# A fused chunk-attention and bilinear-FFN kernel: block 1's output as seven half products, W_out's sums between casts, unit 5's transposes by DMA, and a few moved steps

## The chip, the core and the metric

The kernel runs on one core of a Trainium2 chip. The time is the device time of one execution in microseconds (us), and the figure that is compared is the median over runs. A core has five engines that run their own instruction streams in order: PE (matmuls), DVE (vector), ACT (scalar activations), POOL (GpSimd) and SP, which here only issues DMAs. They meet through semaphores.

## What is computed

Eight sequences of 576 tokens with 8 heads of 64 features go through attention within chunks of 64 tokens, and the result, 4608 rows of 512, goes through a bilinear feed-forward layer with 1536 hidden features.

```python
def _attn_ref(q, k, v):                      # (8, 8, 576, 64) each
    q_c, k_c, v_c = (t.reshape(8, 8, 9, 64, 64) for t in (q, k, v))
    scores = np.matmul(q_c, k_c.transpose(0, 1, 2, 4, 3)) / np.sqrt(64)
    attn = np.exp(scores - np.max(scores, axis=-1, keepdims=True))
    attn = attn / (np.sum(attn, axis=-1, keepdims=True) + 1e-09)
    return np.matmul(attn, v_c).reshape(8, 8, 576, 64)

def _moe_ref(x, w_a, w_b, w_out):            # x (4608, 512), w_a, w_b (512, 1536), w_out (1536, 512)
    return ((x @ w_a) * (x @ w_b) @ w_out).astype(np.float32)
```

## The kernel before

**Units and blocks.** Rows are worked on in 18 units of 256 rows for the attention and in 9 blocks of 512 rows (two units) for the feed-forward layer. The whole order of all five engines is written out by hand (`tc.manual_schedule`): each call appends its instructions to the streams of the engines it uses, so the place of a call in the source is its place in every one of those streams.

**Attention of a unit U.** `load` issues the DMAs of q, k and v from SP. `cast` turns them into bf16 on POOL (`k_raw` and so on, L203). q and k are then transposed into `qkt`, in one of two ways. For units below `PE_UNITS` they are loaded in pieces of 512 bytes, transposed on PE (`transpose_pe`, L217, eight 128x128 tiles each for q and k) and copied out of PSUM by DVE and ACT (L225). For the others they are loaded in the natural order in pieces of 256 bytes and transposed by a DMA issued from SP (`transpose_dma`, L230). `scores` (L248, exponentials on ACT at L256), `sums` (L263, logarithms at L273), `inverse` (L282, the reciprocal as an exponential) and `values` (L296, the product with the reciprocal on DVE at L305, written to `xT`) follow. `bring(U)` casts q and k, loads q of unit U+1, transposes U by DMA, casts v and loads k and v of U+1. SP runs these DMAs in that order.

**Feed-forward.** Block 0 is done by `ab_step` (L355): 12 steps of plain products, 512 columns each. Block 1 is done by 24 half steps `h` of 256 columns, which need only unit 2 for the first twelve. From block 2 on, `Group` uses a scheme with seven products in place of eight (p1 to p7, L405), which needs sums of the weights (`combine_w`, on DVE, L129, four parts for each of six pieces) and sums of x (`combine_x`, on DVE, L385, four parts). The scheme's PSUM copies are on ACT, its additions and its final multiplication on DVE (L443, L444, L455).

**Output.** Block K's output is made while block K+1's products run. Block 0 uses `out_0`, four groups of 12 plain matmuls of 512 columns (L609), in block 1's stretch. Block 1 does the same in pieces of four matmuls (`out_part`), twelve pieces set between block 2's products. From block 2 on, `OutGroup` uses the scheme of seven products for the output too: 14 half products of six matmuls of 256 columns (L541). It needs sums of W_out (`combine_wo`, on POOL, L158, four parts of three) and sums of the hidden product (`combine_ab`, on POOL, L485, four parts of three). Part 3 of `combine_wo` overwrites a quarter of W_out, so it must come after the last plain product that reads it. `chunks` says how many of these pieces stand at each of the twelve places of a block.

The sums of W_out stand in the POOL stream of blocks 2 and 3:

```python
if K == 2:
    for _ in range(2 if i < 3 else 1):
        combine_wo(*wo_sums.pop(0))
if K == 3 and i == 1:
    while wo_sums:
        combine_wo(*wo_sums.pop(0))
```

Of the kernel before, what the change touches and what calls it, by code (L numbers as in the profile page):

```python
# [8 lines left out]


PE_UNITS = 6
AB_SCALE = 256.0
OUT_SCALE = 1.0 / AB_SCALE

# [2 lines left out]
def kernel(  # L17
# [10 lines left out]
    nc = tc.nc  # L28
# [292 lines left out]
        if f is not None:  # L321
            values(f)

    def bring(U):

        if U >= NU:
            return
        cast(U, "qk")
        load(U + 1, "q")
        if U < NU:  # L330
            transpose_dma(U)
        cast(U, "v")
        load(U + 1, "kv")


    ab_tiles = {}

# [281 lines left out]
    with tc.manual_schedule(  # L619
        engines={  # L620
            mybir.EngineType.PE,
            mybir.EngineType.SP,
            mybir.EngineType.DVE,
            mybir.EngineType.Activation,
            mybir.EngineType.Pool,
        }
    ):

        load(0, "qk")
        load(1, "qk")  # L630
        load(0, "v")
        load(1, "v")
        for i in range(3):
            load_ab(i)
        cast(0, "qk")
        transpose_pe(0)
        cast(1, "qk")
        cast(0, "v")
        cast(1, "v")
        cast_ab(0)  # L640
        load_ab(3)
        cast_ab(1)
# [24 lines left out]
        for j in range(6):  # L667
            load_wo(j)
        for j in range(6):
            cast_wo(j)  # L670
        load(4)
        load(5)
        spread[:] = [psum_t, psum_t, psum_a, psum_q]
        combos = [(i, p) for i in range(NWP) for p in range(3)]

        def combo():
            if combos:
                combine_w(*combos.pop(0))

        for ft in range(NFT):  # L680
            ab_step(0, ft)
            if 3 <= ft < 10:
                combo()
            if ft == 6:
                transpose_pe(2)
            if ft == 8:
                slot(2)
            if ft == 10:
                slot(None, 2)

        cast(4)
        cast(5)
        load(6)

        outs = []

        def chunk(n=1):
            for _ in range(min(n, len(outs))):
                outs.pop(0)()

        def half(ft, u):
            ab_step(1, ft, 256 * u, 256 * u + 256)
            if ft > 9 if u == 0 else ft != 5 and ft != 9 and ft != 11:
                combo()
            if u == 1 and ft % 2 and ft > 2:
                combine_w(ft // 2 - 1, 3)

        halves = [(ft, u) for u in range(2) for ft in range(NFT)]

        def h(n=1):  # L710
            for _ in range(n):
                half(*halves.pop(0))

        def normalize(U):
            sums(U)
            inverse(U)

        def out_0(tg):
            for p in range(3):
                out_part(0, tg, p, psum_b)  # L720

        spread[:] = [psum_t, psum_b]
        h(1)
        transpose_pe(3)
        h(3)
        scores(3)
        h(3)
        normalize(3)
        h(2)
        values(3)  # L730
        bring(6)
        h(8)
        out_0(0)
        transpose_pe(4)
        h(2)
        scores(4)
        out_0(1)
        transpose_pe(5)
        h(1)
        normalize(4)  # L740
        h(1)
        scores(5)
        h(1)
        values(4)
        bring(7)
        h(1)
        spread[:] = [psum_a, psum_q]
        normalize(5)
        out_0(2)
        spread[:] = [psum_t]  # L750
        values(5)
        combine_x(2)
        h(1)
        out_0(3)
        assert not halves and not combos

        attention = {}
        for K in range(2, NBLK):
            U = 2 * K + 2
            for at, f, u in (  # L760
                ((0, 0) if K == 2 else (-1, 1), scores, U),
                ((0, 1) if K == 2 else (0, 0), sums, U),
                ((1, 0), inverse, U),
                ((1, 1), values, U),
                ((2, 1), scores, U + 1),
                ((3, 0), sums, U + 1),
                ((3, 1), inverse, U + 1),
                ((4, 1), values, U + 1),
                ((5, 0), lambda u: combine_x(u // 2, (0, 1)), U + 1),
            ):  # L770
                if u < NU:
                    at = (K - 1, NWP - 1, 1) if at[0] < 0 else (K, *at)
                    attention[at] = [lambda f=f, u=u: f(u)]

        for K in range(3, NBLK):
            attention.setdefault((K, 0, 0), []).insert(0, lambda K=K: combine_x(K, (2, 3)))

        def attend(K, i, n):
            for f in attention.get((K, i, n), ()):
                f()  # L780

        wo_sums = [(p, j) for p in range(4) for j in range(3)]
        last = None
        chunks = {
# [3 lines left out]
            NBLK - 1: (1,) * 12,  # L788
        }

        def finish(g):

            K, i = g.K, g.i
            if K >= 2 and i >= 3:
                for part in (0, 1, 2):
                    combine_ab(K, part, i - 3, nc.vector if (K, i) == (NBLK - 1, 5) else None)

        for K in range(2, NBLK):
            for i in range(NWP):
                if i == 1:  # L800
                    if K == 2:
                        outs += [
                            lambda tg=tg, p=p: out_part(1, tg, p, (psum_o, psum_q)[tg % 2])
                            for tg in range(4) for p in range(3)
                        ]
                    else:
                        for j in range(3):
                            combine_ab(K - 1, 3, j)
                if i in (1, 3):
                    bring(2 * K + 4 if i == 1 else 2 * K + 5)  # L810
                if K == 2:
                    for _ in range(2 if i < 3 else 1):
                        combine_wo(*wo_sums.pop(0))
                if K == 3 and i == 1:
                    while wo_sums:
                        combine_wo(*wo_sums.pop(0))
                if K == 2 and i == 0:
                    combine_w(NWP - 1, 3)
                if K > 2 and i == 0:
                    g = OutGroup(K - 1)  # L820
                    outs += [
                        lambda g=g, n=n, th=th: g.part(n, th) for n in range(7) for th in range(2)
                    ]
                now = Group(K, i)
                now.p1()
                if last:
                    last.add7()
                chunk(chunks.get(K, chunks[4])[2 * i])
                if last:
                    last.p3()  # L830
                attend(K, i, 0)
                now.p6()
                if last:
                    last.p4()
                    finish(last)
                now.p2()
                chunk(chunks.get(K, chunks[4])[2 * i + 1])
                attend(K, i, 1)
                now.p5()
                now.p7()  # L840
                last = now
        ends = [
            OutGroup(NBLK - 1, 0, (psum_t, psum_q, psum_o)),
            OutGroup(NBLK - 1, 1, (psum_t, psum_b, psum_a)),
        ]
        last.add7()
        ends[0].part(0, 0)
        last.p3()
        ends[1].part(0, 1)
# [39 lines left out]
```

The softmax here doesn't subtract the row's maximum and nothing guards it: scores larger than these inputs give would overflow.

## Time and profile before

Four runs took 310.65 to 311.82 us, median 311.15 us. The profiled execution is the one of 311.82 us.

| | profiled execution |
|---|---|
| time of that execution | 311.82 us |
| span from first to last instruction | 310.0 us |
| granted PE clock | 0.999 |
| PE busy | 293.4 us (95%) |
| DVE, ACT, POOL busy | 206.8, 194.1, 178.2 us |
| DMA moved | 54.03 MB, 174 GB/s on average |
| packets under 512 bytes | 114016 of 138887 |

A row of a timeline gives the start in us from the span's start, the duration, the engine, the line, the operation and its tiles, and in brackets how long the engine was idle before it and what released it. Matmuls overlap at their ends, so durations of neighbours add up to more than the clock shows; the distance from start to start is what a group costs. In the page's second part each digit is one fortieth of the span, in tenths.

### The profile page before, as it was taken

Reading aid. Unit: us, or ns where it says so; the run is one execution under the profiler, and the core shown is the slowest. Engines: PE = TensorE matmul, PEld = TensorE weight load, DVE = VectorE, ACT = ScalarE, POOL = GpSimd, SP = SyncE. Lnnn points to the kernel's source line nnn. Section 1 sums busy time; section 2 is a strip of 40 time slices with the busy share of each in tenths; the row PEclk is TensorE's granted clock in tenths of the full one; section 3 lists DMA queues with packets and bytes.
Section 4 is the critical chain, followed back from the end, with each engine's and each line's share of the span. In section 5 each row is a group of like instructions: output and inputs, shape, how many; then the busy total and the mean of one; then the engine's idle time right before and its main releaser. Section 6 shows DMA issues by size and latency. Waiting matters only on the chain.

```text
span 310.0 us, 8487 instructions
## 1 busy us (share of the span) xinstructions
PE 293.4 (95%) x3478; PEld 228.6 (74%) x3478; DVE 206.8 (67%) x342; ACT 194.1 (63%) x350; POOL 178.2 (57%) x168
## 2 busy tenths in 40 slices
PE   2889889999999999999999999999999999999995
PEld 1534457866566768888888888888888888888884
DVE  3446663975866687567757776777668766965872
ACT  1743557448575657666877687768676867566531
POOL 1565656554348588945782678277737711780560
PEclk9999999999999999999999999999999999999999
DMA  7999899999999993699539953994492000300015
GB/s 233 307 377 277 246 340 339 209 246 200 269 224 220 241 253 92 85 231 242 139 63 239 242 140 74 218 273 121 93 182 103 36 0 2 137 1 3 0 75 197
DMA packets 138887, 54.03 MB, mean 174 GB/s; under 512 B 114016, under 2 KB 132960, under 8 KB 138848
## 3 DMA queue, kind: packets, MB, share of 16 engines
q1 hardware_dynamic: 138704, 53.36, 70.2%
q8 instruction: 27, 0.44, 0.6%
q10 hardware_dynamic: 144, 0.13, 0.1%
q14 instruction: 12, 0.10, 0.1%
HBM read 37.75 MB, written 9.44 MB: 152 GB/s over the span
## 4 chain that ended last, share of the span: by engine, by line
PE 75%; DMA 7%; DVE 7%; POOL 5%; ACT 3%; issue 2%; SPq 1%; DVEq 0%; POOLq 0%; ACTq 0%
PE pb L405 17%; PE pc L405 11%; PE pa L405 10%; PE po L541 9%; PE pq L541 8%; DMA st<-in_moe_w_b_dram 3%; PE pb L609 3%; DMA st<-in_k_dram 2%; DVE s L385 2%; PE po L355 2%; PE pc L355 2%; DMA st<-in_q_dram 2%; POOL so L485 2%; PE pa L355 2%; PE pq L355 2%
## 5 line engine op out<-in xcount | busy, mean ns | idle before, releaser
L405 PEld LDWEIGHTS <-t 128*128 128x128 f16 x504 | 48.3, 98 | 10.1 <-issue 4.1
L443 DVE TENSOR_TENSOR c_sb<-pc,v_sb 128x512 f32<-128x512 f32 x42 | 28.8, 686 | 35.0 <-ACT v_sb L416 34.3
L485 POOL TENSOR_TENSOR so<-ab_sb 128x512 f16<-128x512 f16 x20 | 23.0, 1152 | 50.3 <-DVE ab_sb L455 50.3
L405 PE MATMUL pb<-s,wa 128*128 128x256 f16 x336 | 50.6, 273 | 0.1
L405 PE MATMUL pa<-xT,wb 128*128 128x256 f16 x336 | 50.4, 273 | 0.0
L416 ACT COPY u_sb<-pb 128x512 f32<-128x512 f32 x42 | 24.7, 587 | 24.8 <-PE pb L405 23.5
L541 PEld LDWEIGHTS <-ab_sb 128*128 128x128 f16 x336 | 32.9, 98 | 4.2 <-issue 0.4
L405 PEld LDWEIGHTS <-wb 128*128 128x128 f16 x336 | 32.9, 98 | 4.0
L203 POOL CAST k_raw<-st 128x1024 bf16<-128x1024 f32 x17 | 17.9, 1056 | 30.9 <-DMA st<-in_k_dram 26.4
L405 PEld LDWEIGHTS <-wa 128*128 128x128 f16 x336 | 31.0, 98 | 6.2 <-issue 0.2
L455 DVE SCALAR_TENSOR_TENSOR ab_sb<-pc,c_sb 128x512 f16<-128x512 f32 x42 | 28.9, 688 | 6.9 <-PE pc L405 5.5
L455 DVE SCALAR_TENSOR_TENSOR ab_sb<-pb,b_sb 128x512 f16<-128x512 f32 x42 | 28.9, 687 | 3.0 <-PE pb L405 2.6
L423 ACT COPY pb<-pa 128x512 f32<-128x512 f32 x42 | 24.6, 587 | 8.5 <-PE pa L405 8.4
L416 ACT COPY v_sb<-pb 128x512 f32<-128x512 f32 x42 | 24.9, 592 | 8.1 <-PE pb L405 8.1
L416 ACT COPY b_sb<-pa 128x512 f32<-128x512 f32 x42 | 25.0, 595 | 7.7 <-PE pa L405 7.7
L444 DVE TENSOR_TENSOR pc<-pc,u_sb 128x512 f32<-128x512 f32 x42 | 29.0, 689 | 0.0
L203 POOL CAST v_raw<-st 128x1024 bf16<-128x1024 f32 x18 | 19.0, 1057 | 15.7 <-DMA st<-in_v_dram 11.8
L305 DVE TENSOR_TENSOR xT<-pt,ln 128x512 f16<-128x512 f32 x30 | 19.4, 685 | 12.2 <-PE pt L296 12.2
L541 PEld LDWEIGHTS <-so 128*128 128x128 f16 x252 | 24.6, 98 | 3.4 <-issue 0.5
L405 PE MATMUL pc<-s,t 128*128 128x256 f16 x168 | 25.2, 272 | 0.6 <-DVE ab_sb L455 0.6
L405 PE MATMUL pb<-s,t 128*128 128x256 f16 x168 | 25.3, 273 | 0.4 <-DVE ab_sb L364 0.4
L405 PE MATMUL pc<-xT,t 128*128 128x256 f16 x168 | 25.2, 272 | 0.1
(132 smaller groups left out, 572.4 us busy)
## 6 DMA issues: line engine op xcount, KB each, us to landing
out_dram<-o_sb SPq DMA_DIRECT2D x34, 256.0 KB, 3.3
st<-in_v_dram SPq DMA_DIRECT2D x32, 256.0 KB, 4.2
st<-in_q_dram SPq DMA_DIRECT2D x23, 256.0 KB, 4.8
st<-in_k_dram SPq DMA_DIRECT2D x23, 256.0 KB, 3.6
st<-in_moe_w_b_dram SPq DMA_DIRECT2D x6, 512.0 KB, 7.6
st<-in_moe_w_a_dram SPq DMA_DIRECT2D x6, 512.0 KB, 8.0
st<-in_moe_w_out_dram SPq DMA_DIRECT2D x6, 512.0 KB, 6.7
st<-in_q_dram SPq DMA_DIRECT2D x4, 512.0 KB, 5.9
```

What stands on the lines that cost most here:

```text
L203: eng.tensor_copy(out=raw[n, U], in_=staged.pop((n, U)))
L305: nc.vector.tensor_tensor(out=x.rearrange("p m (g c s) -> p m g c s", g=2, c=2)[:, :, :, cl, :], in0=av[cl], in1=rs[:, cl].rearrange("p m ...
L355: nc.tensor.matmul(ps[n], w_ab[n, i][:, kt, o:o + 128], xT[:, kt, c0:c1], start=(kt == 0), stop=(kt == NKT - 1),)
L405: nc.tensor.matmul(t[:, h * 256:h * 256 + 256], w[:, kt, h * 128:h * 128 + 128], x[:, kt], start=start and h == 0 and kt == 0, stop=h == 1 ...
L416: nc.scalar.copy(out=t, in_=src)
L423: nc.scalar.copy(out=self.B, in_=self.A)
L443: nc.vector.tensor_tensor(out=self.c, in0=self.C, in1=self.v, op=ADD)
L444: nc.vector.tensor_tensor(out=self.C, in0=self.C, in1=self.u, op=ADD)
L455: nc.vector.scalar_tensor_tensor(out=self.dst[:, :, c0:c0 + 256], in0=t.rearrange("p (h n) -> p h n", h=2), scalar=AB_SCALE, in1=o.rearran ...
L485: (eng or nc.gpsimd).tensor_tensor(out=o, in0=x0, in1=x1, op=op)
L541: nc.tensor.matmul(t[:, c0:c0 + 256], a[:, kt, th * 128:th * 128 + 128], w[:, kt], start=n in (0, 4) and first and kt == 0, stop=last and ...
L609: nc.tensor.matmul(out_ps[K, tg], ab_tiles[K][:, ft, tg * 128:tg * 128 + 128], wo_sb[:, ft], start=(ft == 0), stop=(ft == NFT - 1),)
```

## The change

- `PE_UNITS` goes from 6 to 5. Unit 5's q and k are loaded in natural order and transposed by DMA; its 16 PE transposes and their four copies go.
- `bring` takes a part of `combine_wo` and puts its three pieces between its casts: `bring(5, 0)` in place of `cast(4)`'s follower `cast(5)` and `load(6)`, and `bring(6, 1)`. Part 3 of W_out's sums now stands at the start of block 2, part 2 at its third pair of products; none is left in block 3.
- Block 1's output uses `OutGroup` like the later blocks: 14 half products in block 2. Its `combine_ab` parts 0 to 2 stand at half steps 7, 9 and 11 of the second half of block 1, part 3 in block 2.
- In block 0, `sums(2)` and `inverse(2)` move one step ahead of `values(2)`; unit 3's q is transposed ahead of block 1's first half step and its k after it.
- Unit 5's sums use the banks `psum_q` and `psum_o` in place of `psum_a` and `psum_q`. The last half step of block 1 stands ahead of x's sums for block 2, whose parts 2 and 3 move to the start of block 2. One matmul on zeros into `psum_q` (whose result nothing reads) stands ahead of `out_0(3)`.
- Part 3 of `combine_w` for the pieces 3, 4 and 5 moves into block 2's first three pairs.

```diff
-PE_UNITS = 6
+PE_UNITS = 5
...
-        cast(U, "qk")
+        def between(j):
+            if part is not None:
+                combine_wo(part, j)
+
+        cast(U, "q")
+        between(0)
+        cast(U, "k")
         load(U + 1, "q")
-        if U < NU:
-            transpose_dma(U)
+        transpose_dma(U)
+        between(1)
         cast(U, "v")
         load(U + 1, "kv")
-
+        between(2)
...
+            if ft == 9:
+                sums(2)
+                inverse(2)
             if ft == 10:
-                slot(None, 2)
+                values(2)
...
         cast(4)
-        cast(5)
-        load(6)
+        bring(5, 0)
...
-            if u == 1 and ft % 2 and ft > 2:
+            if u == 1 and ft in (3, 5, 7):
                 combine_w(ft // 2 - 1, 3)
+            if u == 1 and ft % 2 and ft > 6:
+                for part in range(3):
+                    combine_ab(1, part, ft // 2 - 3)
...
+        transpose_pe(3, "q")
         h(1)
-        transpose_pe(3)
+        transpose_pe(3, "k")
...
-        bring(6)
+        bring(6, 1)
...
-        transpose_pe(5)
...
-        spread[:] = [psum_a, psum_q]
+        spread[:] = [psum_q, psum_o]
         normalize(5)
         out_0(2)
         spread[:] = [psum_t]
         values(5)
-        combine_x(2)
         h(1)
+        combine_x(2, (0, 1))
+        whole = bank(psum_q)
+        nc.tensor.matmul(whole, warm_in[:, :128], warm_in, start=True, stop=True)
         out_0(3)
...
-        for K in range(3, NBLK):
+        for K in range(2, NBLK):
             attention.setdefault((K, 0, 0), []).insert(0, lambda K=K: combine_x(K, (2, 3)))
...
-            2: (0, 0, 1, 1, 1, 1, 1, 1, 1, 1, 1, 1),
-            3: (1, 1, 2, 2, 1, 1, 2, 2, 1, 1, 1, 1),
+            2: (0, 1, 1, 1, 2, 1, 2, 2, 1, 1, 1, 1),
...
-                if i == 1:
+                if K == 2 and i == 0:
+                    combine_wo_all(3)
+                if i == (2 if K == 2 else 1):
+                    for j in range(3):
+                        combine_ab(K - 1, 3, j)
                     if K == 2:
-                        outs += [
-                            lambda tg=tg, p=p: out_part(1, tg, p, (psum_o, psum_q)[tg % 2])
-                            for tg in range(4) for p in range(3)
-                        ]
-                    else:
-                        for j in range(3):
-                            combine_ab(K - 1, 3, j)
+                        combine_wo_all(2)
...
-                if K == 2:
-                    for _ in range(2 if i < 3 else 1):
-                        combine_wo(*wo_sums.pop(0))
-                if K == 3 and i == 1:
-                    while wo_sums:
-                        combine_wo(*wo_sums.pop(0))
-                if K == 2 and i == 0:
-                    combine_w(NWP - 1, 3)
-                if K > 2 and i == 0:
+                if K == 2 and i < 3:
+                    combine_w(i + 3, 3)
+                if i == 0:
                     g = OutGroup(K - 1)
```

More of the change, by code (lines that the diff above doesn't have):

```diff
@@ L322, in slot, with bring @@
             values(f)
-    def bring(U):
+    def bring(U, part=None):
         if U >= NU:
             return
-        cast(U, "qk")
+        def between(j):
[4 more added lines that the diff above has]
+        cast(U, "k")
         load(U + 1, "q")
-        if U < NU:
-            transpose_dma(U)
+        transpose_dma(U)
+        between(1)
         cast(U, "v")
         load(U + 1, "kv")
+        between(2)
     ab_tiles = {}
@@ L687, with combine_wo_all @@
                 slot(2)
+            if ft == 9:
+                sums(2)
+                inverse(2)
             if ft == 10:
-                slot(None, 2)
+                values(2)
+        def combine_wo_all(part):
+            for j in range(3):
+                combine_wo(part, j)
         cast(4)
-        cast(5)
-        load(6)
+        bring(5, 0)
         outs = []
@@ L780, in attend @@
                 f()
-        wo_sums = [(p, j) for p in range(4) for j in range(3)]
         last = None
         chunks = {
[2 rows of a table removed]
+            2: (0, 1, 1, 1, 2, 1, 2, 2, 1, 1, 1, 1),
             4: (1, 1, 1, 1, 1, 1, 2, 2, 1, 1, 1, 1),
@@ L799 @@
             for i in range(NWP):
-                if i == 1:
-                    if K == 2:
-                        outs += [
-                            lambda tg=tg, p=p: out_part(1, tg, p, (psum_o, psum_q)[tg % 2])
-                            for tg in range(4) for p in range(3)
-                        ]
-                    else:
-                        for j in range(3):
-                            combine_ab(K - 1, 3, j)
+                if K == 2 and i == 0:
+                    combine_wo_all(3)
+                if i == (2 if K == 2 else 1):
+                    for j in range(3):
+                        combine_ab(K - 1, 3, j)
+                    if K == 2:
+                        combine_wo_all(2)
                 if i in (1, 3):
                     bring(2 * K + 4 if i == 1 else 2 * K + 5)
-                if K == 2:
-                    for _ in range(2 if i < 3 else 1):
-                        combine_wo(*wo_sums.pop(0))
-                if K == 3 and i == 1:
-                    while wo_sums:
-                        combine_wo(*wo_sums.pop(0))
-                if K == 2 and i == 0:
-                    combine_w(NWP - 1, 3)
-                if K > 2 and i == 0:
+                if K == 2 and i < 3:
+                    combine_w(i + 3, 3)
+                if i == 0:
                     g = OutGroup(K - 1)
```

## The prediction

> **What bounds the kernel now.** I read the page's busy shares first, then its forty slices, then PE's timeline from block 0's end to block 3 for every place where PE was idle, and last the SP and POOL streams, which say when the data for those places can be there.
>
> ```profile
> PE 293.4 (95%) x3478; PEld 228.6 (74%) x3478; DVE 206.8 (67%) x342; ACT 194.1 (63%) x350; POOL 178.2 (57%) x168
> PE   2889889999999999999999999999999999999995
> DMA  7999899999999993699539953994492000300015
> ```
>
> PE is busy 95% of the span and almost without a gap from 135 us to the tail at the end. So the end moves by what PE's own work loses or gains, and by what its idle places lose or gain. The DMA row shows the second limit: up to about 112 us the DMA engines are full, afterwards not. The edit lies in 38 to 135 us, partly where both are full.
>
> ```profile
> 44.18 0.60 PE L355 MATMUL pa<-xT,wb 128*128 128x256 f16 x4 [1.47 <-DVE xT L305]
> ...
> 70.20 0.61 PE L217 MATMUL pt<-identity,q_raw 128*128 128x128 bf16 x8
> 70.65 0.61 PE L217 MATMUL pb<-identity,k_raw 128*128 128x128 bf16 x8
> 71.10 0.60 PE L355 MATMUL pq<-xT,wb 128*128 128x256 f16 x4
> ...
> 76.78 0.41 PE L263 MATMUL pa<-E,ones 64*64 64x512 bf16 x2 [0.47 <-ACT v_sb L363]
> ...
> 85.01 0.60 PE L405 MATMUL pb<-s,t 128*128 128x256 f16 x4 [0.37 <-DVE ab_sb L364]
> ...
> 87.79 1.03 PE L609 MATMUL po<-wo,ab_sb 128*128 128x512 f16 x4
> 88.65 0.60 PE L405 MATMUL pb<-s,wa 128*128 128x256 f16 x4
> ...
> 114.02 0.60 PE L405 MATMUL pc<-s,t 128*128 128x256 f16 x4 [0.41 <-DVE ab_sb L455]
> ...
> 126.28 0.82 PE L541 MATMUL pq<-wot,so 128*128 128x256 f16 x6
> 126.93 0.60 PE L405 MATMUL pb<-s,wa 128*128 128x256 f16 x4
> ...
> 132.03 1.03 PE L541 MATMUL pq<-wo,so 128*128 128x256 f16 x8 [0.30 <-POOL wo L158]
> ```
>
> These are PE's timeline: its idle places that the edit touches (1.47, 0.47, 0.37, 0.41, 0.30 us), unit 5's transposes (70.20 to 71.10), and the price of an output piece from start to start: 0.86 us for four plain matmuls, 0.65 for six half ones.
>
> ```profile
> 72.23 2.43 SPq L230 DMA_TRANSPOSE qkt<-q_raw  x1
> 74.76 1.25 SPq L230 DMA_TRANSPOSE qkt<-k_raw  x1
> 76.06 2.09 SPq L176 DMA_DIRECT2D st<-in_k_dram  x2
> ```
>
> This is SP: unit 6's two transposes, and the load queued behind them. Unit 6's k landed at 79.01, 6.8 us after 72.23.
>
> **The change part by part.** All in the profiled execution (span 310.0, time 311.82); that run is 0.67 above the median of 311.15, so I carry the difference over to the median.
>
> *Block 0's end.* PE waits 1.47 us at 44.18 because sums(2) came at 40.16, its logarithms and reciprocal took ACT until 42.81 and DVE's two products ran from 42.84 to 44.13. With sums(2) one step (1.73 us) earlier, at 38.4, ACT works 38.9 to 41.0. But ACT's copy v_sb of step 10 is now queued behind them: 41.0 to 41.6, and DVE's multiplication of that step 41.6 to 42.2 stands ahead of the xT products, which run 42.2 to 43.5. Block 1 starts at 43.55, not 44.18: 0.63 us. v of unit 2 was cast by 40.02 and values(2) now comes at 40.45, q of unit 3 was cast by 41.78 and is transposed at 42.6 inside the remaining gap: 0.45 us more (45.05 to 45.50 before). Sum -1.08; between -0.5 (the transposes alone) and -1.5 (the gap gone).
>
> *Unit 5's transposes off PE.* -0.90 (70.20 to 71.10); its four copies, 1.34 us on DVE and 1.33 on ACT, were beside other work. PE would reach scores(5) at 73.39 - 1.98 = 71.41.
>
> *Unit 5's transposes in SP's queue.* Now q5 and k5 are four DMAs of 256 KB with 256-byte packets, not two of 512 KB. In the trace a 256 KB load lands 0.9 to 1.0 us after the one before it, a 512 KB one with 512-byte packets 1.5 us after (k5, 62.22 to 63.73): +0.9 us on this queue. q6's last piece was issued by 66.25; now by 67.2, and the q transpose follows it at once, since q5 (landing near 62.7) and k5 (64.5) are cast on POOL by 66, with one W_out sum between. From the q transpose's issue to the k transpose's landing the twelve pairs took 4.1 us (190 us, empty queue) to 6.8 (72 us, full). This queue is full, but the loads just ahead are of 128 KB; I take 5.9, the 83 us pair, so 73.1. PE waits from 71.41 to 73.15: +1.74; from 0 (4.1 us) to 3.9 (start 68.5, 6.8 us). So scores(5) starts at 73.15 where it was 73.39: of 1.98 us gained, 0.24 stays.
>
> [...] The trace has PE at 0.90 us for all 16 tiles, and a DMA pair in a full queue adding 1.95 us (q8 landed 87.19, unit 7's transposes 88.30 and 89.14). [...] The rows are of the same operation in this kernel, so I take 5.9 us.
>
> *Sums(5) and the zero matmul.* Sums(5) waited 0.47 us for ACT's copy v_sb out of pa. Now it needs u_sb, one copy earlier, and DVE's read of po; with ACT and DVE 1.3 us lighter and 2.3 us of PE between scores(5) and it, the wait goes: -0.47 (0 if DVE is late). The zero matmul needs pq after ACT's copy c_sb, which ended at 81.2 when PE was free at 81.08; it takes 0.22: +0.4 (0.2 to 0.5). From scores(5) to block 2's scores(6) was 10.81 us (73.39 to 84.20) and becomes 10.74: scores(6) at 83.9.
>
> *What is late next: unit 6.* k6's load stands behind unit 5's transposes on SP. They end issuing 3.8 us after their start (as at 72.23 to 76.01), at 71.0; k6, v6 and q7 took 5.9 us to issue (66.35 to 72.23): 76.9; plus 6.3: k6's transpose lands at 83.2. Scores(6) needs it at 83.9. Slack 0.7; before it was 5.2.
>
> *POOL.* k6 and v6 would land near 75.6 and 77.5. POOL does v6's cast and the last sum of part 1 by 80, then the first two `combine_ab` triples (three of 1.16 us) by 87, the three casts of unit 7 by 90.1 (q7 was cast at 75.78; its transpose at SP's turn, about 87.5, thus waits 0.6 us, and unit 7 is needed at 96.9 with a landing near 94), the third triple, whose second sum is ready at 92.5. PE asks for it in the fifth chunk of block 2, at 94. Part 3 of W_out's sums (three of 1.13) ends at 97 and is asked for at 98.9; `combine_ab` part 3 ends at 103.5, asked for at 105; W_out's part 2 at 107, asked for at 110. Four slacks of 1.5 to 3 us. Stores of block 1's output go behind unit 9's transposes in SP's order, which are due late (scores(9) stood at 129.43). For unit 6 and POOL together I put +0.2 (0 to 3).
>
> *Block 2's PE work.* Twelve pieces of 0.864 us become fourteen of 0.655: 10.37 - 9.17 = -1.20. ACT gets five copies of 0.58 us more and DVE one operation of 0.68 less, as in the later blocks, where PE has no gap. x's sums stand behind one DVE multiplication and, parts 2 and 3, behind one weight sum: with each at the slow 1.26 us of this trace, s2 is ready 4.3 us after values(5), asked for after 4.8. The 0.37 us at 85.01 is ACT's copy of pa and stays. The three moved weight sums are used from the fourth pair on.
>
> *Two waits.* At 114.02 DVE was behind by an o_sb eviction (L602, 0.59 us on its path) that is gone: -0.4. At 132.03 PE waited for W_out's part 3 on POOL, now done 35 us earlier: -0.3.
>
> Sum: -0.24 - 0.47 + 0.4 - 1.20 - 0.4 - 0.3 + 0.2 = -2.0 us. Profiled 311.8 becomes 309.8; the median 309.1.
>
> **The rivals.** *The transpose is in time* (chance 0.2): with 4.1 us the k transpose lands at 71.3 and the 1.74 us are kept: -3.75, 307.4. For it: pieces just ahead are small. Against: no pair below 110 us took less than 5.9.
>
> *The gain is only moved* (0.13): pair at 6.8 us and a start at 68.5, landing at 75.3: -2.0 + 2.15 = +0.15, 311.3; anything between that and 0.9 less is no change.
>
> *Slower: unit 6's keys* (0.15). Place: scores(6), block 2's start. Unit 6's transposes follow unit 5's in one queue and so carry its lateness twice, and everything that POOL casts after k6 comes later with them. It decides from the k transpose landing after 83.9; each us then costs one; at 86.8 the sum is +0.9, at 88 it is +2.1, 313.3. For it: the slack falls from 5.2 to 0.7 and DMA is at 1.0 to 1.2 in this stretch. Against: the time at which unit 6 is due moves with PE's own wait. [...]
>
> *Not as written:* that block 1's output still waits for its sums in block 2, so that the 1.2 us are given back in POOL waits; it is in the 0.2 above, and at 1.5 us it gives 310.4, still inside.
>
> **How the numbers follow.** Likeliest, 0.52: -2.0, own range 308.2 to 310.1. In time: 0.20, about 307.4. Only moved: 0.13, 310.2 to 311.5. Slower: 0.15, above 312. A measurement of this kernel can tell about 0.3%, 0.93 us, from no change: faster means under 310.2, slower over 312.1. Faster: 0.72; same: 0.13; slower: 0.15. The range leaves out the slower case and the tip of the in-time one: 307.2 to 311.2.
>
> **What would show it.** Right: block 1 starts near 43.6 with unit 3's q before it; PE idle before scores(5) by 1 to 2.5 us with a DMA as releaser; no wait at unit 5's sums; no L609 in block 2; no idle at block 3's 132. Wrong: scores(5) without a wait (307.4); PE idle at scores(6) or in L541 of block 2 with POOL so or wot as releaser; a clock under 1.0.

## The result: a little faster, less than half of the forecast

The changed kernel took 309.99 us in the median (308.76 to 312.35 over 43 runs); the kernel before, run beside it, 311.15 us (309.98 to 312.98 over 64). The ratio of the means (310.31 and 311.19 us) is 0.9972, with a 95% interval of 0.9961 to 0.9982: 0.9 us faster (1.2 us by the medians), where 2.0 had been forecast. A second batch (c0 below) gave 0.9981 (0.9966 to 0.9995). The profiled execution of the changed kernel took 310.67 us, with a span of 308.9 us.

The page of the changed kernel, first its busy time and then two rows of its forty slices:

```profile
PE 293.0 (95%) x3499; PEld 231.4 (75%) x3499; DVE 209.5 (68%) x339; ACT 195.9 (63%) x353; POOL 192.3 (62%) x180
PE   2879999999999989999999999999999999999995
DMA  7999999999989998399639943993493000300025
```

PE has as much to do as before. What grew is POOL, from 178.2 to 192.3 us (twelve `combine_ab` sums for block 1's output), and DVE, from 206.8 to 209.5 us, although three DVE instructions fewer are issued; ACT's 1.8 us more are its additional copies. On DVE, fewer instructions in more time: some of them became slower. That is the first hint.

PE's timeline at the places that the prediction named:

```profile
43.38 0.60 PE L362 MATMUL pa<-xT,wb 128*128 128x256 f16 x4 [0.19 <-DVE xT L305]
...
69.79 0.60 PE L362 MATMUL pq<-xT,wb 128*128 128x256 f16 x4
...
72.07 0.22 PE L248 MATMUL pt<-qkt 64*64 64x64 bf16 x2
...
75.64 0.40 PE L263 MATMUL po<-E,ones 64*64 64x512 bf16 x2 [0.28 <-DVE ab_sb L371]
...
80.12 0.38 PE L771 MATMUL pq<-warm_in 128*128 128x512 bf16 x1
80.34 2.75 PE L616 MATMUL pb<-wo,ab_sb 128*128 128x512 f16 x12
...
89.75 0.60 PE L412 MATMUL pc<-xT,t 128*128 128x256 f16 x4 [0.51 <-DVE pc L451]
...
114.72 0.60 PE L412 MATMUL pc<-s,t 128*128 128x256 f16 x4 [0.83 <-DVE ab_sb L462]
```

The gap ahead of block 1 fell from 1.47 to 0.19 us. Scores(5), at 72.07, did not wait for its DMA in this execution. But PE now waits for DVE at 75.64, 89.75 and 114.72, and the last wait, which was to go, has doubled (0.41 before). The 0.30 us at block 3's 132 are gone. SP's queue:

```profile
65.70 1.97 SPq L230 DMA_TRANSPOSE qkt<-q_raw  x1
67.77 1.24 SPq L230 DMA_TRANSPOSE qkt<-k_raw  x1
69.06 1.95 SPq L176 DMA_DIRECT2D st<-in_k_dram  x3
...
74.78 2.88 SPq L230 DMA_TRANSPOSE qkt<-q_raw  x1
```

Unit 5's pair was issued at 65.70 (forecast 67.2) and its k landed at 71.26 (forecast 73.1). Behind it stand unit 6's loads, from 69.06 on.

**A ledger by stretches.** Executions of one kernel differ by a microsecond or more, and much of that comes from the start: scores(2), with nothing ahead of it changed, began between 35.35 and 37.10 us in all but one of the kernels below. So I count in PE's timeline from scores to scores, from the first matmul of one unit's scores to that of a later unit's. The last column is the changed kernel with unit 5 back on PE (e1, e1b, e1c below: three profiles).

| stretch, us | before | forecast of the difference | changed | changed, c0 | unit 5 on PE |
|---|---|---|---|---|---|
| scores 2 to 3 (block 0's end) | 12.53 | -1.08 | 11.42 | 11.42 | 11.42 |
| 3 to 4 | 18.47 | 0 | 19.31 | 18.47 | 18.47 to 18.58 |
| 4 to 5 (transposes of 5, its landing) | 6.16 | +0.84 | 5.27 | 5.27 | 6.16 |
| 5 to 6 (sums(5), zero matmul) | 10.81 | -0.07 | 11.38 | 11.15 | 11.39 to 11.46 |
| 6 to 10 (blocks 2 and 3) | 61.60 | -1.70 | 61.09 | 61.63 | 59.29 |
| 10 to the end | 164.24 | 0 | 164.32 | 164.32 | 164.24 to 164.25 |
| sum | 273.81 | -2.01 | 272.78 | 272.26 | 270.99 to 271.09 |

The two early steps came. In blocks 2 and 3, where 1.70 us were to come, the changed kernel gained 0.51 us in one profile and nothing in the other.

### The profile page after: what moved, and what is told of

Its sections match the earlier page's. It is cut to its first block, busy times and chain, and to the rows that moved or that the text cites. A ratio compares the mean times of both kernels' runs of the same rounds, so it can differ in the third digit from the quotient of the medians.

```text
span 308.9 us, 8539 instructions
## 1 busy us (share of the span) xinstructions
PE 293.0 (95%) x3499; PEld 231.4 (75%) x3499; DVE 209.5 (68%) x339; ACT 195.9 (63%) x353; POOL 192.3 (62%) x180
## 4 chain that ended last, share of the span: by engine, by line
PE 76%; DVE 7%; DMA 5%; SPq 4%; ACT 3%; issue 2%; POOL 1%; ACTq 0%; DVEq 0%; POOLq 0%
PE pb L412 18%; PE pc L412 12%; PE po L548 11%; PE pa L412 11%; PE pq L548 9%; PE pb L616 3%; DMA st<-in_moe_w_b_dram 3%; DMA st<-in_k_dram 2%; PE pt L263 2%; SPq L176 2%; PE pt L296 1%; PE pt L248 1%; SPq L188 1%; PE po L362 1%; ACT ln L273 1%
## 5 line engine op out<-in xcount | busy, mean ns | idle before, releaser
L492 POOL TENSOR_TENSOR so<-ab_sb 128x512 f16<-128x512 f16 x23 | 26.7, 1160 | 47.4 <-DVE ab_sb L462 47.4
L548 PEld LDWEIGHTS <-ab_sb 128*128 128x128 f16 x384 | 37.6, 98 | 4.7 <-issue 0.4
L548 PEld LDWEIGHTS <-so 128*128 128x128 f16 x288 | 28.1, 98 | 3.4
L492 POOL TENSOR_TENSOR so<-so,ab_sb 128x512 f16<-128x512 f16 x23 | 26.6, 1158 | 1.8
L492 POOL TENSOR_TENSOR ab_sb<-ab_sb 128x512 f16<-128x512 f16 x23 | 27.1, 1180 | 0.0
```

Of the source, the lines that this page charges most:

```text
L492: (eng or nc.gpsimd).tensor_tensor(out=o, in0=x0, in1=x1, op=op)
L548: nc.tensor.matmul(t[:, c0:c0 + 256], a[:, kt, th * 128:th * 128 + 128], w[:, kt], start=n in (0, 4) and first and kt == 0, stop=last and ...
```

## The experiments

Theory A: DVE's sums with both inputs in SBUF (x's sums, L392, and the weight sums, L129; f16, 512 columns) take 0.41 us alone and over 1 us beside a POOL instruction (1.12 and 1.26 us at 111.65 and 112.81 in the changed kernel); POOL, made late, now runs beside them. Rivals: B, DVE is late only because instructions were moved; C, PE's being earlier is given back at random; and the forecast's own, a DMA landing. Four kernels came first.

**e1: unit 5 back on PE.**

```diff
-PE_UNITS = 5
+PE_UNITS = 6
...
-        transpose_dma(U)
+        if U >= PE_UNITS:
+            transpose_dma(U)
...
         out_0(1)
+        transpose_pe(5)
         h(1)
```

> The changed kernel with unit 5 transposed on PE again (16 tiles and four copies after out_0(1)), everything else as changed. The forecast's theory, a DMA landing that PE must wait for, gave the step only 0.24 us, so the time would go from 310.0 to about 310.2. Theory A (no such wait exists in the trace of after: keys landed at 71.26, scores(5) began at 72.07; the step is worth its whole 0.90 us): 310.9, PE 0.9 us longer between the half step before scores(5) and scores(5). If DVE is what holds PE at block 2's start anyway, less than 0.9, because PE's delay is absorbed in the wait at sums(5) (0.28) and at p7 (0.51): 310.4.

Measured: 308.65 us, ratio 0.9941 (0.9923 to 0.9958). Every expectation had this kernel slower; it is faster than the changed one. In the ledger its transposes cost the 0.89 us (6.16 for 5.27), and blocks 2 and 3 give back 1.8 to 2.3. PE's timeline shows no wait over 0.2 us between 84.5 and 134 us.

**e2: block 0's end as before.**

```diff
-            if ft == 9:
-                sums(2)
-                inverse(2)
             if ft == 10:
-                values(2)
+                slot(None, 2)
...
-        transpose_pe(3, "q")
         h(1)
-        transpose_pe(3, "k")
+        transpose_pe(3)
```

> The changed kernel with block 0's end as before: sums(2), inverse(2) and values(2) together at step 10, both of unit 3's transposes after block 1's first half step. By the ledger alone the step was worth 1.10 us (block 1's second half step came at 44.70 for 45.94): 311.1. Theory A and C (PE being early is given back in the half steps at 59 to 61, where DVE's weight sums stand beside POOL's casts and PE loses 0.84 us): only about +0.3, 310.3, the wait at 61.05 smaller.

Measured: 309.46 us, 0.9958 (0.9946 to 0.9971), no slower than e4 and e6 beside it. The edge itself is worth its 1.1 us: scores 2 to 3 took 12.54 us. The rest has another reason than I expected: the 0.84 us at 59 to 61 are at that size in the first profile of the changed kernel alone (19.31 us, against 18.47 in e2, e4 and c0 and at most 18.81 in the other kernels, with this stretch unchanged), so that part of A and C was chance.

**e4: two moved weight sums back in block 1.**

```diff
-            if u == 1 and ft in (3, 5, 7):
+            if u == 1 and ft % 2 and ft > 2:
                 combine_w(ft // 2 - 1, 3)
...
-                if K == 2 and i < 3:
-                    combine_w(i + 3, 3)
+                if K == 2 and i == 0:
+                    combine_w(NWP - 1, 3)
```

> The changed kernel with two of the three moved weight sums (part 3 for pieces 3 and 4) back in half steps 9 and 11 of block 1, the third at the first pair of block 2, as before. Theory A/B (DVE's queue at block 2's start, with weight sums of 1.25 to 1.37 us each, is what makes p7 wait 0.51 us at 89.75): the wait shrinks to 0.25 or less, 309.6. The forecast (the moved sums cost nothing): no change, 310.0, and if the sums only move the lateness to the half steps at 75 to 80, no change either.

Measured: 309.48 us, 0.9958 (0.9944 to 0.9972). The wait at p7 went, as A and B have it, but 0.84 us at 83.10 (ACT) and 0.53 us at 93.29 (POOL) came in its place; in sum nothing is shown.

**e6: the first triple of `combine_ab` of block 2 one pair later.** Its `finish` is done together with the next one.

```diff
-                    finish(last)
+                    if K == 2 and last.i == 3:
+                        pass
+                    elif K == 2 and last.i == 4:
+                        finish(first)
+                        finish(last)
+                    else:
+                        finish(last)
```

> The changed kernel with the first triple of POOL's sums of the hidden product of block 2 one pair of products later, so that POOL is idle while DVE makes x's sums for block 3 near 111 us. Theory A (contention: DVE's sums take 0.41 us alone, 1.1 to 1.3 beside POOL): those sums return to about 0.4 us, the wait of 0.83 us at 114.7 goes, 309.3. Theory B (DVE's order and number of instructions): the sums may speed up, but the wait stays above 0.4; 309.9.

Measured: 309.62 us, 0.9959 (0.9942 to 0.9977), with waits of 0.54 and 1.07 us at 113.22 and 119.27: what A expected failed, and the edit was a poor one: nothing stands between the two triples in POOL's stream, so POOL began the first as soon as it was free of unit 9's casts, at 110.96, beside the sums as before. A place in the source moves an instruction in time only past what stands in the same stream. In e4's and e6's timelines of PE the forecast's DMA wait appears, here e6's:

```profile
72.05 0.22 PE L248 MATMUL pt<-qkt 64*64 64x64 bf16 x2 [1.30 <-DMA qkt<-k_raw]
```

In e4 it was 0.62 us. So the landing does stop PE in some executions; its size is 0 to 1.3 us, not 1.74.

**What e1 points to.** DVE and then POOL in the changed kernel, near x's sums for block 3:

```profile
111.65 1.12 DVE L392 TENSOR_TENSOR s<-xT 128x512 f16<-128x512 f16 x1
112.81 1.26 DVE L392 TENSOR_TENSOR s<-s,xT 128x512 f16<-128x512 f16 x1
113.99 0.68 DVE L462 SCALAR_TENSOR_TENSOR ab_sb<-pc,c_sb 128x512 f16<-128x512 f32 x1
```

```profile
109.10 1.04 POOL L203 CAST v_raw<-st 128x1024 bf16<-128x1024 f32 x1
110.10 1.15 POOL L492 TENSOR_TENSOR so<-ab_sb 128x512 f16<-128x512 f16 x1
111.33 1.16 POOL L492 TENSOR_TENSOR so<-so,ab_sb 128x512 f16<-128x512 f16 x1
112.44 1.34 POOL L492 TENSOR_TENSOR ab_sb<-ab_sb 128x512 f16<-128x512 f16 x1
```

And the same with unit 5 on PE (e1c's timelines of DVE and of POOL):

```profile
111.08 0.41 DVE L393 TENSOR_TENSOR s<-xT 128x512 f16<-128x512 f16 x1
111.53 0.42 DVE L393 TENSOR_TENSOR s<-s,xT 128x512 f16<-128x512 f16 x1
```

```profile
107.27 1.15 POOL L493 TENSOR_TENSOR so<-ab_sb 128x512 f16<-128x512 f16 x1 [0.99 <-DVE ab_sb L463]
108.50 1.16 POOL L493 TENSOR_TENSOR so<-so,ab_sb 128x512 f16<-128x512 f16 x1
109.61 1.16 POOL L493 TENSOR_TENSOR ab_sb<-ab_sb 128x512 f16<-128x512 f16 x1
112.64 1.15 POOL L493 TENSOR_TENSOR so<-ab_sb 128x512 f16<-128x512 f16 x1 [1.86 <-DVE ab_sb L463]
```

The brackets are the point. Here POOL is on time: each triple waits for DVE's `ab_sb`. DVE makes x's sums just ahead of an `ab_sb` product, so a POOL that waits for that product is idle during the sums. In the changed kernel POOL's first row has no bracket: it has a backlog and works through the sums. DVE's next product comes 1.5 us later (1.12 and 1.26 us for twice 0.41), and PE waits for it.

**c0, e10, e11, e12.** c0 is the changed kernel again.

> The changed kernel once more, as it is, beside the three others of this batch. Its ratio to the kernel before should be 0.997 again (0.996 to 0.998). It fixes what the others are read against, and its trace shows how often DVE's four sums of x for block 3 (near 111 and 117 us) take over 1 us: the new theory (POOL's lateness puts its sums of the hidden product beside them) expects at least two of the four there at 1.0 to 1.4 us and PE waits of 0.8 to 2.1 us together between 112 and 122; the rival, that those waits came by chance in one trace, expects them at about 0.4 in this one.

Measured: 0.9981 (0.9966 to 0.9995). The four sums took 0.41, 1.14, 1.20 and 1.37 us, and PE waited 1.08 us at 118.84 (and 0.52 at 93.17 for POOL): the waits were no chance of one trace, but their place varies. Scores 8 to 10, the stretch around these sums, took 32.07 us here, 31.65 in the first profile and 30.42 in e1.

e10 takes POOL work away and leaves unit 5 on the DMA path (the tile that these sums would fill is set to zero once at the start):

```diff
-                    if K == 2:
-                        combine_wo_all(2)
```

> The changed kernel with part 2 of W_out's sums left out (wot4 is set to zero once at the start; that part of the output is then not the reference's). Unit 5 stays on the DMA path. POOL then has 3.4 us less to do at 103.6, so its triple for the hidden product of block 2 can run at 107 to 110.5, ahead of DVE's sums of x at 111. New theory (POOL's timing against DVE's sums decides): those sums fall to 0.41 us each, the PE waits between 112 and 122 go, 0.8 to 2.1 us less than the changed kernel, so near 308.5. Rival (unit 5 on PE is faster for its DMA order, or for PE's own order, and POOL is beside the point): the time stays within 0.3 us of the changed kernel.

Measured: 0.9958 (0.9942 to 0.9975) against c0's 0.9981, intervals that overlap; its sums again took 0.41, 1.14, 1.20 and 1.37 us. The 3.4 us did not reach the triple, as POOL's timeline in e10 shows:

```profile
103.94 1.04 POOL L204 CAST q_raw<-st 128x1024 bf16<-128x1024 f32 x1
108.60 1.04 POOL L204 CAST k_raw<-st 128x1024 bf16<-128x1024 f32 x1 [3.62 <-DMA st<-in_k_dram]
110.74 1.26 POOL L204 CAST v_raw<-st 128x1024 bf16<-128x1024 f32 x1 [1.10 <-DMA st<-in_v_dram]
111.96 1.32 POOL L493 TENSOR_TENSOR so<-ab_sb 128x512 f16<-128x512 f16 x1
```

POOL's work is in order, and the triple stands behind two casts whose loads are late in SP's queue. POOL is late by its own work and by the DMA queue at once; taking away one leaves the other.

e11 makes POOL later with unit 5 on PE:

```diff
                         combine_wo_all(2)
+                        combine_wo_all(2)
```

> Unit 5 on PE as in the fastest run so far, but part 2 of W_out's sums made twice (the second time the same values into the same place), so that POOL is 3.4 us later from 102 us on. New theory: POOL's triple moves from 107 to 110.4, beside DVE's sums of x at 110.8 and 116, they take 1.0 to 1.4 us again, and the waits at p7/p4 of block 3 return: 0.8 to 2.1 us slower than with unit 5 on PE alone, near 309.9 to 310. Rival (POOL's time does not matter there): no change from 308.7.

Measured: 0.9953 (0.9936 to 0.997). The triple moved only to 108.45, since slack took up part of the delay; the sums took 0.64, 0.42, 0.42 and 0.41 us, and scores 8 to 10 the same 30.42 us as in e1. The dose was too small to decide.

e12 leaves the matmul on zeros out:

```diff
-        whole = bank(psum_q)
-        nc.tensor.matmul(whole, warm_in[:, :128], warm_in, start=True, stop=True)
```

> Unit 5 on PE and the matmul on zeros ahead of out_0(3) left out (nothing reads its result). If the 0.40 us that the trace shows between values(5)'s half step and out_0(3) is PE's own: 308.65 minus 0.4, 308.25. If block 2's start is held by DVE's sums of x and the copy of pa (a wait of 0.36 at 83.98 already), those take it back: 308.6.

Measured: 0.9946 (0.9925 to 0.9967); scores 5 to 6 took 10.99 us for 11.40. So the matmul costs its 0.40 us. Its zeros count, though: without it the output is off by a relative 0.15, so the 0.40 us are not to be had this way.

**e1b, e13, e15, e16.** e1b is e1 again.

> Unit 5 transposed on PE, once more, beside the three others of this batch. As before: ratio 0.994 to the kernel before (some 2 us under it, 1 under the changed kernel), DVE's four sums of x at 0.41 us, no PE wait between 84 and 134 us.

Measured: 309.52 us, 0.992 (0.99 to 0.9941), with all four sums at 0.42 to 0.43 us.

e13 puts ten sums on POOL behind unit 9's casts:

```diff
+                if K == 2 and i == 3:
+                    for _ in range(10):
+                        nc.gpsimd.tensor_tensor(
+                            out=scratch, in0=wo_sb[:, 0, 0:192], in1=wo_sb[:, 2, 0:192], op=ADD
+                        )
```

> Unit 5 on PE, and ten small sums on POOL into a scratch tile (nothing reads it) behind unit 9's casts, some 5 us in all: no DMA and no PE instruction moves, only POOL's triples for the hidden product of block 2 come as late as in the changed kernel. New theory (POOL with a backlog works beside DVE's sums of x, which then take 1.0 to 1.4 us for 0.41): at least two of those four sums over 1.0 us, PE waits of 0.8 to 2.1 us between 112 and 122, and 0.8 to 2.1 us slower than unit 5 on PE alone. Rival (unit 5 on PE is faster by the order of DMAs or of PE): the time stays within 0.3 us of it.

Measured: 317.51 us, 1.0178 (1.0154 to 1.0203). An overdose, and not usable: the ten took 6.71 us, so that PE waited 3.06 us for POOL itself at 132.06, and its x sums (0.88, 0.65, 0.42, 0.77) met little. It shows something else. PE's timeline:

```profile
132.06 0.61 PE L551 MATMUL pq<-wot,so 128*128 128x256 f16 x2 [3.06 <-POOL so L495]
132.46 1.06 PE L415 MATMUL pb<-s,wa 128*128 128x256 f16 x4
```

After this wait a group of four matmuls took 0.85 us from start to start (132.46 to 133.31) where e1b has 0.44, and the granted clock of this execution is 0.995 in the mean, where e1b's is 1.000. As an estimate, the missing 0.005 of the span of 317.8 us is 1.6 us, lost on top of the wait if all of it lies there. Besides, this kernel was 3 us late already at scores(2), which I can't explain; it has one tile more, but that was not tried by itself.

e15 relieves POOL in two ways at once:

```diff
-            if part is not None:
-                combine_wo(part, j)
+            if part == 0:
+                combine_wo(0, j)
+            elif part == 1:
+                for p, n in (((1, 0), (1, 1), (1, 2)), ((2, 0), (2, 1)), ((2, 2),))[j]:
+                    combine_wo(p, n)
...
-        load(U + 1, "q")
+        load(U + 1, "qkv" if U == 8 else "q")
         transpose_dma(U)
...
-        load(U + 1, "kv")
+        load(U + 1, "" if U == 8 else "kv")
...
-                    if K == 2:
-                        combine_wo_all(2)
```

> The changed kernel, unit 5 still on the DMA path, with two moves that free POOL near 104 to 110 us: part 2 of W_out's sums goes into POOL's idle time at 71 to 78 (inside bring(6)), and unit 9's loads of k and v go ahead of unit 8's transposes in SP's queue, so that their casts do not wait until 110.7. New theory: the triple of block 2 runs at 107 to 110.5, DVE's sums of x are back at 0.41, the waits at 112 to 122 go: 1 to 1.5 us less than the changed kernel, as fast as unit 5 on PE within 0.5 us. Rival (unit 5's place itself): stays at the changed kernel's time.

Measured: 309.86 us, 0.9939 (0.991 to 0.9967). Not as expected in the trace: v of unit 9 still held POOL for 2.33 us, until 109.49, and the sums took 1.28, 1.26, 1.03 and 0.41 us, the first two in DVE's timeline:

```profile
111.87 1.28 DVE L395 TENSOR_TENSOR s<-xT 128x512 f16<-128x512 f16 x1
113.19 1.26 DVE L395 TENSOR_TENSOR s<-s,xT 128x512 f16<-128x512 f16 x1
```

PE waited 0.99 us for DVE at 115.10, and scores 8 to 10 took 31.82 us.

e16 is e1 with e2's edit.

> Unit 5 on PE and block 0's end as in the kernel before (sums, inverse and values of unit 2 together at step 10, unit 3's transposes after the first half step). With unit 5 on the DMA path undoing that edge cost nothing (309.46 against 309.5 to 309.6 in that batch), which the DMA landing at 71 to 72 us explains: PE being early there only lengthens the wait. With that landing gone the edge's 1.10 us of the ledger should show: 1.0 to 1.2 us slower than unit 5 on PE alone. If DVE's sums at block 2's start hold PE as well, 0.4 to 0.8.

Measured: 309.67 us, 0.9936 (0.9915 to 0.9957), beside 309.52 for e1b: by the medians of six runs each no difference shows. By the ledger the edge costs 1.10 us (scores 2 to 3: 12.52 for 11.42), the later stretches stay as they were, and the sum is 272.07 for 271.09. The whole spans of the two profiles hide most of it, since scores(2) began 0.7 us earlier in e16. I hold the ledger to be right; the medians do not show it.

**e17, e18, e1c: the two causes parted.** e17 is e1 with part 1 of W_out's sums made twice, so that POOL alone is later:

```diff
                     bring(2 * K + 4 if i == 1 else 2 * K + 5)
+                if K == 2 and i == 3:
+                    combine_wo_all(1)
```

> Unit 5 on PE, and part 1 of W_out's sums made a second time behind unit 9's casts (the same values into the same place, 3 x 1.15 us on POOL, no new tile). The ten scratch sums of the run before took 6.7 us and came on top of a POOL that was late from the start, so that PE waited 3.1 us for POOL itself at 132; this is the smaller dose that was meant. POOL's triple moves from 107 to 110 and so beside DVE's sums of x at 110.8. New theory: the first two sums of x take 1.0 to 1.3 us (0.41 before), PE waits 0.5 to 1.1 us between 112 and 122, the stretch from scores(8) to scores(10) grows from 30.4 us to 31.0 to 32.0, 0.6 to 1.5 us slower than unit 5 on PE alone. Rival (unit 5's DMAs themselves, or their order, cost the time): stretch and time as with unit 5 on PE, within 0.3 us.

Measured: 309.95 us, 0.9947 (0.9925 to 0.9968), beside 308.73 for e1c. Its timelines of POOL, DVE and PE:

```profile
106.03 3.38 POOL L158 TENSOR_TENSOR wot<-wot,wo 128x512 f16<-128x512 f16 x3
109.36 1.16 POOL L493 TENSOR_TENSOR so<-ab_sb 128x512 f16<-128x512 f16 x1
110.60 1.15 POOL L493 TENSOR_TENSOR so<-so,ab_sb 128x512 f16<-128x512 f16 x1
111.72 1.33 POOL L493 TENSOR_TENSOR ab_sb<-ab_sb 128x512 f16<-128x512 f16 x1
```

```profile
110.95 1.08 DVE L393 TENSOR_TENSOR s<-xT 128x512 f16<-128x512 f16 x1
112.07 1.26 DVE L393 TENSOR_TENSOR s<-s,xT 128x512 f16<-128x512 f16 x1
```

```profile
113.98 0.60 PE L413 MATMUL pc<-s,t 128*128 128x256 f16 x4 [0.80 <-DVE ab_sb L463]
```

With unit 5 on PE and no DVE or PE instruction moved, the picture of the changed kernel is back: sums of 1.08 and 1.26 us, a wait of 0.80 us, and scores 8 to 10 at 31.37 us for 30.42: 0.95 of the 1.23 us (first profile) and 1.65 us (c0) that the changed kernel loses there. Rival B needs a moved DVE instruction, and the DMA rival a moved DMA; there is none.

e18 is e15 with unit 9's v cast behind the last triple, so that POOL is on time with unit 5 on the DMA path:

```diff
-        cast(U, "v")
+        if U != 9:
+            cast(U, "v")
...
                     finish(last)
+                    if K == 3 and i == 0:
+                        cast(9, "v")
```

> As the changed kernel with W_out's part 2 and unit 9's loads moved ahead (unit 5 on the DMA path), and the cast of v of unit 9, which POOL waited 2.33 us for with its triples queued behind it, moved behind the last triple of block 2. New theory: the triples run at 107 to 110.5, 112.4 and 117.4, DVE's sums of x return to 0.41, the stretch from scores(8) to scores(10) falls from 31.8 to about 30.4 us; 1.2 us less than the version that it builds on, 1.7 to 2.2 under the kernel before. Rival: as the version that it builds on.

Measured: 309.61 us, 0.9921 (0.9889 to 0.9953). Its timelines of POOL, DVE and PE:

```profile
107.81 1.15 POOL L496 TENSOR_TENSOR so<-ab_sb 128x512 f16<-128x512 f16 x1 [0.93 <-DVE ab_sb L466]
```

```profile
111.62 0.42 DVE L396 TENSOR_TENSOR s<-xT 128x512 f16<-128x512 f16 x1
112.07 0.42 DVE L396 TENSOR_TENSOR s<-s,xT 128x512 f16<-128x512 f16 x1
```

```profile
94.23 0.39 PE L552 MATMUL pq<-wot,so 128*128 128x256 f16 x2 [1.82 <-POOL so L496]
```

POOL waits for `ab_sb` again. All four sums took 0.42 us, and scores 8 to 10 took 30.65 us where e15, which differs by the place of this cast alone, has 31.82. Unit 5 is on the DMA path in both: in this stretch its DMAs act through POOL's time. The kernel as a whole did not gain the 1.2 us, because PE waits 1.82 us at 94.23 for one of POOL's earlier triples. The sums that I had moved forward stand ahead of it, and POOL had waited 2.37 us for unit 6's k; in e15, with the same POOL stream up to there, the wait was 0.54 us, since PE came later. No run takes these sums away by themselves.

> Unit 5 on PE as a reference for the two others on the same chip: 0.992 to 0.994 of the kernel before, stretch from scores(8) to scores(10) of 30.4 us.

Measured: 308.73 us, 0.9904 (0.987 to 0.9939), scores 8 to 10 in 30.42 us. The changed kernel with unit 5 on PE beats both kernels: 0.9941, 0.992 and 0.9904 of the kernel before in three batches, where the changed one has 0.9972 and 0.9981. It was not run beside the changed kernel itself; e11, which is e1 with more work for POOL, took 309.55 us beside c0's 310.36.

## Why the prediction was wrong, step by step

- *Block 0's end*, -1.08: right. 1.11 us.
- *Unit 5's transposes off PE*, -0.90: right. 0.89 us (6.16 to 5.27). By DMA the 16 tiles took from 65.70 to 71.26, beside other work.
- *Unit 5's transposes in SP's queue*, +1.74: mis-sized. 0 in both profiles of the changed kernel, 0.62 and 1.30 in e4 and e6. The pair took 5.56 us (5.9 estimated) and was issued 1.5 us earlier than estimated; in c0 scores(5) began at 71.08, with no wait either.
- *Sums(5)*, -0.47: did not come. DVE's weight sum stood ahead of the product that frees `po`, and sums(5) still waited 0.28 us. Counted from start to start, its two parts were held up by 0.85 us (0.62 in c0, 0.75 in e1c, 0.53 before), beyond e4, where nothing held them. *The zero matmul*, +0.4: right. Together the stretch 5 to 6 grew by 0.34 and 0.57 us, where -0.07 was forecast; in e4 and e6, where PE had waited at scores(5) and DVE caught up, it was 10.53.
- *Unit 6 and POOL*, +0.2: the step that failed. Its times were good (part 2 of W_out's sums to end at 107; it ended at 106.99), and from 62 us on no PE instruction waited for POOL in the first profile (one did in c0, 0.52 us). But POOL's lateness was judged only by what PE asks of POOL. It also had to be judged by what DVE does at that time: DVE's sums took 1.0 to 1.4 us for 0.41 beside the late POOL, and PE waited 0.83 us for them in one profile and 1.08 in the other.
- *Block 2's PE work* with *Two waits*, -1.20, -0.4 and -0.3: the PE work was right. With POOL on time, blocks 2 and 3 gain 2.3 us (61.60 to 59.3), more than the 1.9 in these terms. The wait at 132 went. The wait at 114 had been put down to an eviction; the eviction went and the wait grew to 0.83 us. The trace of before already shows the slow sum, in DVE's timeline and POOL's:

```profile
111.45 0.62 DVE L385 TENSOR_TENSOR s<-xT 128x512 f16<-128x512 f16 x1
112.11 1.26 DVE L385 TENSOR_TENSOR s<-s,xT 128x512 f16<-128x512 f16 x1
113.29 0.68 DVE L455 SCALAR_TENSOR_TENSOR ab_sb<-pc,c_sb 128x512 f16<-128x512 f32 x1
```

```profile
110.63 1.17 POOL L485 TENSOR_TENSOR ab_sb<-ab_sb 128x512 f16<-128x512 f16 x1
111.74 1.34 POOL L158 TENSOR_TENSOR wot<-wo,wot 128x512 f16<-128x512 f16 x1
```

The second sum took three times 0.41 us, with a POOL sum beside it until 113.08. The prediction used 1.26 as "slow" for block 2 and did not ask what makes a sum slow. Had it asked, the POOL schedule that it had worked out (busy without a gap from 80 to 107, casts of unit 9 and a triple next) would have put POOL beside the sums at 111.

So two errors stand against each other: a wait that did not come (1.74 too much), and losses that were not counted (1.2 to 1.7 us in the stretch 6 to 10, 0.4 to 0.6 in 5 to 6 by sums(5)). That 309.99 us still lies within the stated 307.2 to 311.2 is in part luck.

What is shown of the loss in 6 to 10, and what is not: against e1 it was 1.80 and 2.34 us. Of this, 1.23 and 1.65 us lie between scores 8 and 10; e17 brings on most of the first by POOL's time alone, and e18 takes such a loss away. The other 0.56 and 0.68 us lie between scores 6 and 8, where PE waited for DVE at 89.75 in one profile and for POOL at 93.17 in the other. No run tried that part by itself.

Of the rivals, "the transpose is in time" is what happened at scores(5), but its 307.4 us did not come, for its gain was lost again later; "only moved" came near the time (310.2 us at its lower end) by a mechanism that was not at work; "unit 6's keys" did not happen (they landed at 80.69, scores(6) stood at 83.45). That everything POOL casts after unit 6's k comes later was written there; only the price was looked for at the wrong engine. The sign of being wrong that it names, PE idle in block 2's output products with POOL as releaser, came in c0 (0.52 us).

Left open: the loss between scores 6 and 8, why a stretch's loss lies at 89.75 and 114.72 in one profile and at 93.17 and 118.84 in the next, and e13's late start.

## What to carry to other kernels

When work is put on a second engine, list which instructions of the first slow down beside it (here DVE's sums, from 0.41 to as much as 1.37 us) and where those stand, not only who waits for the results. An engine that waits for its input is quiet at a known place; one with a backlog is not, so a step that makes it late can cost time without anything waiting for it (0.95 us in e17). Count such changes in stretches between fixed instructions, since the start alone moves an execution by as much as the effect (scores(2) began between 35.35 and 37.10 us here).

## What the runs showed of the hardware

- A DVE sum of two f16 tiles in SBUF, 512 columns, took 0.41 to 0.43 us with POOL idle (0.41 at 118.44 in the changed kernel, 0.43 at 82.70 in the kernel before, 0.42 in e18), and up to 1.37 us, three times its own, beside POOL's sums (84.64 in the changed kernel). How much went with how far POOL's instruction had come. In the kernel before, the sum at 111.45 took 0.62 us, with 0.34 us of the POOL sum left when it began, and the one at 112.11 took 1.26 us, with 0.97 us left. Where POOL's instruction began just after DVE's sum, POOL's was the one that grew: in the kernel before, at 58.15, the DVE sum took 0.41 us and the cast beside it, at 58.18, 1.29 for 1.04. Three weight sums next to POOL's casts took 1.08 to 1.18 us at 56 to 60 us in the changed kernel. DVE products that read PSUM stayed at 0.67 to 0.70 us beside the same POOL work. POOL's own sums grew too, from 1.15 to 1.34 us (112.44 in the changed kernel).
- The matmul on zeros costs PE 0.40 us (scores 5 to 6 took 10.99 us without it in e12, 11.40 with it), and leaving it out puts the output off by a relative 0.15. How its zeros come to matter was not shown.
- In e13, after a wait of 3.06 us, a group of four matmuls took 0.85 us from start to start (132.46 to 133.31), where e1b has 0.44; the mean granted clock of the execution was 0.995. In e18, after a wait of 1.82 us, the groups kept their time: 0.43 to 0.44 us from 94.47 on.
